# Low-part transposes and row scatters of a chunk, put off by one to three steps, in a scan with a mixture of experts

## The chip, the cores and the metric

One core of one Trainium2 chip. The metric is the device time of one execution in microseconds; the time of a kernel is the median of its runs.

## The reference

`x` and `f_logit` are 4 x 5056 x 256. A gated scan runs along each sequence, and its output goes token by token (20,224 of them) through one of eight experts, the one with the largest gate logit:

```python
f = lower_bound + (1 - lower_bound) * sigmoid(f_logit)
h = f[:, t] * h + (1 - f[:, t]) * x[:, t]          # for each t: y[:, t] = h
logits = y @ w_gate                                # 20224 x 8
e = argmax(logits)
gate_w = softmax(logits)[e];  eom = sigmoid(y @ w_output_gate)[e]
out = gate_w * eom * (relu(y @ w1[e]) @ w2[e])     # w1[e]: 256 x 1024, w2[e]: 1024 x 256
```

## The kernel before

**Chunks.** The tokens are taken in 40 chunks of 512 (`chunk`, L259; the last has 256). `load_chunk` (L246) puts f and x, channels on partitions, into two tiles `ft` and `xt`, of which there are two each in turn (`XB`). A chunk computes tanh on ScalarE (L270), the scan on VectorE (L285), a scale, then splits the scanned rows into a high (L315) and a low (L319) fp16 part, both written over `ft`. `turn(i, k)` (L310) issues a DMA transpose on SP's queue that puts 128 channels of one part into `rows`, tokens on partitions: two for the high part (L323), two for the low part (L343). Small matmuls (L334) give the gate logits; VectorE finds each token's expert and its place in that expert's list (L350 to L421) and the factor (L435). Then four indirect DMAs on POOL's queue (L438), one per 128 tokens, scatter the rows to `scr` in device memory, sorted by expert.

**Tiles.** `plan` (L481) turns the counts of tokens already sent into tiles of 256 rows of one expert, whose place and expert are known only at run time. `gather` (L631) fetches one such tile by a DMA transpose on SP into `xq` (L638) and its places and factors into `mt` (L641). `gemm1` (L681) multiplies with w1 in three fp16 products (L690 to L692), `low` (L698) makes the low part of the hidden values on VectorE, `gemm2` (L708) multiplies with w2 (L730 to L732), `evacuate` (L767) scales on ScalarE (L776) and `put` (L778) scatters the result to `out` on POOL (L780). Before these run-time tiles, while the weights are still being prepared, there are sixteen early tiles of known expert.

**The order of the work.** It is written out by hand. `chunk` is a generator; a bare `yield` ends its work for one step, a yield of `SMALL` or `BIG` only lets other work of the same step in between (`together`, L158). `pump` (L841) runs one step: it begins a new chunk every eight steps (`PERIOD`), moves every live chunk one step on, the oldest first, together with the work of the tile, and at most one plan. `experts` (L975) has four quarters to a tile of 256 rows, and each makes one step. `ahead` (L871), called at a tile's first quarter, sees that the next tile is planned and gathered; if no rows are known it plans at once. A chunk counts as sent when its last scatter is issued (`state["sent"]`, L443). `loading` (L799) issues the loads of the next chunk after a chunk's fifth bare yield. `aside` and `beside` (L232, L237) put the chunk's small matmuls between the tile's.

`between["on"]` is set (L1020) when the run-time tiles begin. From there on `ordered` (L965) keeps every engine's instructions in the order in which they are written. SP's queue is in that order throughout. A DMA waits only for what its data need, so before the change a transpose goes when its part is written, and the scatters one after another when the places are known.

Of the kernel before, what the change touches and what calls it, by code (L numbers as in the profile page):

```python
# [12 lines left out]
I16 = mybir.dt.int16  # L13
# [7 lines left out]
DATA = mybir.DependencyInfo(mybir.DependencyClass.Sync, mybir.DependencyReason.DATA)  # L21
# [17 lines left out]
PUMPS0 = 3.0  # L39
TURN = 3  # L40
XB = 2
DRAIN = 1.25
REST = 6

# [6 lines left out]
def raw(ins):  # L51
    return getattr(ins, "ins", ins)
# [3 lines left out]
def tile_scan_moe(  # L56
# [10 lines left out]
    nc = tc.nc  # L67
    P = 128
    D, N = xT.shape
    KD = D // P  # L70
# [18 lines left out]
    def sure(tokens):  # L89
# [19 lines left out]
        out=tri, in_=ones, compare_op=ALU.is_gt, fill=0.0, base=0, pattern=[[1, P]], channel_multiplier=-1  # L109
# [63 lines left out]
    def alone(g):  # L173
# [12 lines left out]
        out=gsq, in0=wgf, scalar=1.0, in1=wgf, op0=ALU.mult, op1=ALU.mult, accum_out=gss  # L186
# [9 lines left out]
        out=wgs[:, :, 1, :], in0=wgc, scalar=gsc, in1=wgs[:, :, 0, :], op0=ALU.mult, op1=ALU.subtract  # L196
# [5 lines left out]
    def apart(ins, group, keep=()):  # L202
        tc.declare_no_dep(raw(ins), group=group, keep=[raw(k) for k in keep], reason="rows apart")
        tc.add_to_no_dep_group(group, raw(ins))
# [25 lines left out]
    between = {"on": False}  # L230

    def aside(f, *a):  # L232
        queue.append((f, a))
        if not between["on"]:
            beside()
# [10 lines left out]
    def load_chunk(c):  # L246
# [5 lines left out]
        else:  # L252
            ft = p1.tile([P, KD, CH], F32, tag="ft", name="ft", bufs=XB)
            xt = p1.tile([P, KD, CH], F32, tag="xt", name="xt", bufs=XB)
        nc.sync.dma_start(out=ft[:, :, 0:n], in_=fv_in[:, :, t0 : t0 + n])
        nc.sync.dma_start(out=xt[:, :, 0:n], in_=xv_in[:, :, t0 : t0 + n])
        loaded[c] = (xt, ft)

    def chunk(c):  # L259

        t0 = c * CH
        n = min(CH, N - t0)
        nb = n // P
# [8 lines left out]
        for k in range(KD):  # L272
            yield BIG
            nc.vector.scalar_tensor_tensor(
                out=h[k], in0=f[k], scalar=1.0, in1=h[k], op0=ALU.subtract, op1=ALU.mult
# [5 lines left out]
        for k in range(KD):  # L281
            for a, z in zip(cuts[:-1], cuts[1:]):
# [3 lines left out]
                    out=xt[:, k, a:z], data0=ft[:, k, a:z], data1=xt[:, k, a:z], initial=init, op0=ALU.mult, op1=ALU.add  # L286
# [19 lines left out]
        hl = ft.rearrange("p k n -> p (k n)").bitcast(F16).rearrange("p (i k n) -> p i k n", i=2, k=KD)  # L306
        rows = row2[c % 2] if c else row0
        assert c < 3 or c - 2 in state

        def turn(i, k):  # L310
            q = i * KD + k
            nc.sync.dma_start_transpose(out=rows[:, 0:nb, q * P : (q + 1) * P], in_=hl[:, i, k, 0:n].bitcast(I16))

        for k in range(KD):
            nc.scalar.activation(hl[:, 0, k, 0:n], xt[:, k, 0:n], AF.Copy, scale=sa[:, k : k + 1])  # L315
# [1 line left out]
        for k in range(KD):  # L317
            yield BIG
            nc.vector.scalar_tensor_tensor(  # L319
                out=hl[:, 1, k, 0:n], in0=xt[:, k, 0:n], scalar=sa[:, k : k + 1], in1=hl[:, 0, k, 0:n],  # L320
                op0=ALU.mult, op1=ALU.subtract,
            )
            turn(0, k)  # L323
# [15 lines left out]
        for b in range(nb):  # L339
            for i in range(2):  # L340
                aside(gates, i, b)
        for k in range(KD):
            turn(1, k)  # L343
        yield
        lgp = sp.tile([P, NB, 2 * G], F32, tag="lgp", name="lgp")
        nc.scalar.activation(lgp[:, 0:nb], pr[:, 0:nb], AF.Copy, scale=li)
        yield
        lgo = sp.tile([P, NB, G], F32, tag="lgo", name="lgo")
        yield SMALL
        nc.vector.tensor_tensor(out=lgo[:, 0:nb], in0=lgp[:, 0:nb, 0:G], in1=lgp[:, 0:nb, G : 2 * G], op=ALU.add)  # L350
# [6 lines left out]
        def small(nm, w=None, dt=F32):  # L357
# [11 lines left out]
            out=key[:, 0:nb], in0=dl[:, 0:nb], scalar=0.0, in1=rev.unsqueeze(1).to_broadcast([P, nb, E]),  # L369
# [26 lines left out]
        for s in range(nb + 1):  # L396
# [12 lines left out]
            out=pos[:, 0:nb], in0=pk[:, 0:w].rearrange("p (b e) -> p b e", e=E),  # L409
# [10 lines left out]
        with nc.allow_low_precision("whole numbers"):  # L420
# [9 lines left out]
            out=fc[:, 0:nb], in0=es[:, 0:nb], scalar=1e-9, in1=eg[:, 0:nb], op0=ALU.add, op1=ALU.mult  # L430
# [4 lines left out]
        nc.vector.tensor_scalar(meta[:, :, 0:2].bitcast(F32), fc[:, 0:nb].unsqueeze(2), ix, None, ALU.mult)  # L435
        yield
        for b in range(nb):
            ins = nc.gpsimd.indirect_dma_start(  # L438
                out=scr[:, :], out_offset=IOA(ap=dst[:, b : b + 1], axis=0), in_=rows[:, b, :], in_offset=None
            )  # L440
            apart(ins, "scr")
            fresh.append(ins)
        state["sent"] = cn  # L443
# [355 lines left out]
    def loading(c):  # L799

        at = 0
        for kind in chunk(c):
            if not kind:
                at += 1
                if at == LOADAT and EARLY[0] <= c + 1 < NCH:
                    load_chunk(c + 1)
            yield kind

    def plans(need):
# [12 lines left out]
        if c == NCH:  # L822
            prog["final"] = True
            planning.append(plan(WHOLE, P, P // 2 - 1, "whole"))
            for nm, of in (("hh", "ft"), ("hl", "xt")):
                z = p1.tile([P, KD, CH], F32, tag=of, name=of, bufs=XB).rearrange("p k n -> p (k n)").bitcast(F16)
                z = z.rearrange("p (j i n) -> p j i n", i=2, n=P)
# [32 lines left out]
    def step(k, tasks, need=PLAN):  # L860
        prog["left"] += k
        if prog["left"] < 1.0:
            together(tasks)
        while prog["left"] >= 1.0:
            prog["left"] -= 1.0
            pump(tasks, need)
            tasks = []
# [15 lines left out]
    turns = [0] * len(EARLY)  # L883

    def early(j):

        if not line or line[0]["half"] == 1 and len(line) == 1:
            for r in range(len(firsts)):
                e = turns[r]
                if e < min(E, (j + 1) // 2) and (r == 0 or e < turns[r - 1]):  # L890
                    T = gather(f"f{r * E + e}", firsts[r][e], e)
                    T["half"] = 0
                    line.append(T)
                    turns[r] += 1
                    break
        tasks, wait, ready, late = [], list(pend), list(over), list(mid)
        pend.clear()
        over.clear()
        mid.clear()
        for T, h in wait:  # L900
            tasks.append(first_low(T, h))
            if h == 0:
                tasks.append(factors(T))
        go = line and line[0]["ev"] < j // 2

        def rest():
            for T in ready:
                evacuate(T)
                put(T)
            if go:  # L910
                T, h = line[0], line[0]["half"]
                T["half"] += 1
                if h == 1:
                    line.pop(0)
                first1(T, h)
                pend.append((T, h))
            for T, h in late:
                first2(T, h)
                if h == 1:
                    over.append(T)  # L920
            mid.extend(wait)

        return tasks, rest
# [31 lines left out]
    while turns[-1] < E or line or pend or mid or over:  # L955
        mine, rest = early(nh)
        step(DRAIN, mine, LEAD)
        rest()
# [16 lines left out]
    def experts(t0, t1, more, late=0, rest=None):  # L975
# [3 lines left out]
        for t in range(t0, t1 + 2):  # L979
# [4 lines left out]
            for q in range(4):  # L984
# [12 lines left out]
                if T and t == end - 1 and q % 2:  # L997
                    if q == 1:
                        T["w2"] = [
                            p1.tile([P, KD, CH], F32, tag=of, name=of, bufs=XB).rearrange("p k n -> p (k n)").bitcast(F16)  # L1000
                            for of in ("ft", "xt")
# [74 lines left out]
```

## Time and profile before

| | us |
|---|---|
| median of 3 runs | 999.99 |
| lowest, highest | 997.69, 1004.57 |
| the profiled execution | 999.55 |
| its span, from the first to the last instruction | 997.8 |
| TensorE, VectorE, ScalarE, GpSimd (POOL) busy in it | 913.4, 799.1, 510.8, 361.1 |

Times in the rows are counted from the span's start. A matmul's end is modelled, and matmuls overlap: in a dense row of them one of 256 columns starts every 0.11 us and is shown as 0.27 us long. An idle time in brackets counts from the end of the row before.

### The profile page before, as it was taken

Reading aid. Unit: us, or ns where it says so; the run is one execution under the profiler, and the core shown is the slowest. Engines: PE = TensorE matmul, PEld = TensorE weight load, DVE = VectorE, ACT = ScalarE, POOL = GpSimd, SP = SyncE. Lnnn points to the kernel's source line nnn. Section 1 sums busy time; section 2 is a strip of 40 time slices with the busy share of each in tenths; the row PEclk is TensorE's granted clock in tenths of the full one; section 3 lists DMA queues with packets and bytes.
Section 4 is the critical chain, followed back from the end, with each engine's and each line's share of the span. In section 5 each row is a group of like instructions: output and inputs, shape, how many; then the busy total and the mean of one; then the engine's idle time right before and its main releaser. Section 6 shows DMA issues by size and latency. Waiting matters only on the chain.

```text
span 997.8 us, 30899 instructions
## 1 busy us (share of the span) xinstructions
PE 913.4 (92%) x9775; PEld 817.2 (82%) x9775; DVE 799.1 (80%) x2683; ACT 510.8 (51%) x1075; POOL 361.1 (36%) x380
## 2 busy tenths in 40 slices
PE   2257888999999999999999999999999999999997
PEld 2247868788888888888888888888888888899996
DVE  7978867697888888888888888888888886836653
ACT  6666656454655554555555555545555453333332
POOL 1432324243433434443334444333434343321112
PEclk9669989999999999999999999999999999999999
DMA  8899973886666557567656666656566653232211
GB/s 306 205 272 268 256 199 110 156 174 146 139 152 160 135 151 138 154 146 149 161 132 149 146 155 149 154 144 138 134 152 143 153 126 82 72 88 46 52 34 34
DMA packets 236526, 146.15 MB, mean 146 GB/s; under 512 B 200507, under 2 KB 202172, under 8 KB 236368
## 3 DMA queue, kind: packets, MB, share of 16 engines
q1 hardware_dynamic: 220784, 101.34, 45.9%
q0 software_dynamic: 15296, 42.73, 14.5%
q8 instruction: 93, 1.52, 0.6%
q14 instruction: 65, 0.53, 0.2%
q10 hardware_dynamic: 288, 0.02, 0.0%
HBM read 58.38 MB, written 44.23 MB: 103 GB/s over the span
## 4 chain that ended last, share of the span: by engine, by line
PE 74%; issue 10%; DMA 8%; DVE 4%; POOL 2%; SPq 1%; ACT 0%; another core or an unknown queue 0%; POOLq 0%; DVEq 0%; ACTq 0%
PE ph L690 11%; PE py L730 11%; PE ph L691 11%; PE ph L692 11%; PE py L732 11%; PE py L731 11%; DMA out_dram<-yo,mt 3%; DMA xq<-scr 3%; POOL out_dram L780 2%; PE ph L743 1%; PE ph L744 1%; PE ph L745 1%; PE pr L334 1%; DMA w<-in_wT_dram 1%; PE py L764 1%
## 5 line engine op out<-in xcount | busy, mean ns | idle before, releaser
L695 ACT ACTIVATE hh<-ph 128x512 f16<-128x512 f32 (+1 forms) x312 | 173.3, 556 | 309.9 <-PE ph L692 246.3
L690 PE MATMUL ph<-xq,w 128*128 128x256 f16 (+2 forms) x1312 | 326.1, 259 | 3.2 <-DVE fac L657 2.2
L691 PE MATMUL ph<-xq,w 128*128 128x256 f16 (+2 forms) x1312 | 326.3, 259 | 1.5 <-issue 1.3
L692 PE MATMUL ph<-xq,w 128*128 128x256 f16 (+2 forms) x1312 | 326.6, 259 | 0.7 <-issue 0.4
L730 PE MATMUL py<-w2s,hh 128*128 x1136 | 309.0, 272 | 2.5 <-issue 2.0
L731 PE MATMUL py<-w2s,hh 128*128 x1136 | 309.2, 272 | 0.5 <-issue 0.5
L732 PE MATMUL py<-w2s,hl 128*128 x1136 | 309.3, 272 | 0.0
L780 POOL DMA_INDIRECT out_dram<-yo,mt x146 | 150.3, 1029 | 384.5 <-ACT yo L776 340.0
L703 DVE SCALAR_TENSOR_TENSOR hl<-ph,hh 128x512 f16<-128x512 f32 (+1 forms) x312 | 198.6, 636 | 46.6 <-ACT hh L695 35.9
L438 POOL DMA_INDIRECT scr<-rows,dst x154 | 177.6, 1154 | 142.4 <-issue 128.5
L665 DVE COPY w<-w1s 128x2048 f16 x164 | 114.2, 697 | 51.8 <-PE ph L692 37.5
L690 PEld LDWEIGHTS <-w 128*128 128x128 f16 x1312 | 127.6, 97 | 15.8 <-DVE fac L657 2.5
L692 PEld LDWEIGHTS <-w 128*128 128x128 f16 x1312 | 127.3, 97 | 13.9 <-issue 2.2
L691 PEld LDWEIGHTS <-w 128*128 128x128 f16 x1312 | 127.3, 97 | 11.7 <-issue 2.1
L732 PEld LDWEIGHTS <-hl 128*128 128x128 f16 x1136 | 110.7, 97 | 14.7 <-issue 0.6
L730 PEld LDWEIGHTS <-hh 128*128 128x128 f16 x1136 | 110.8, 98 | 13.7 <-issue 1.7
L731 PEld LDWEIGHTS <-hh 128*128 128x128 f16 x1136 | 110.7, 97 | 11.4 <-issue 0.5
L285 DVE TENSOR_TENSOR_SCAN xt<-ft,xt 128x512 f32<-128x512 f32 (+4 forms) x78 | 92.5, 1195 | 0.3
L776 ACT ACTIVATE yo<-py,fac 128x256 f32<-128x256 f32 (+1 forms) x146 | 62.0, 469 | 30.3 <-PE py L732 25.3
L315 ACT ACTIVATE ft<-xt,sa 128x512 f16<-128x512 f32 (+1 forms) x76 | 50.2, 708 | 43.2 <-DVE pos L408 23.1
L319 DVE SCALAR_TENSOR_TENSOR ft<-xt,sa,ft 128x512 f16<-128x512 f32 (+1 forms) x76 | 56.1, 742 | 20.0 <-ACT ft L270 18.1
L334 PEld LDWEIGHTS <-ft 128*128 128x128 f16 x600 | 51.2, 98 | 17.9 <-ACT ft L315 5.0
(189 smaller groups left out, 1364.6 us busy)
## 6 DMA issues: line engine op xcount, KB each, us to landing
ft<-in_fT_dram SPq DMA_DIRECT2D x37, 512.0 KB
xt<-in_xT_dram SPq DMA_DIRECT2D x37, 512.0 KB
w<-in_wT_dram SPq DMA_DIRECT2D x32, 512.0 KB
scr<-rows,dst POOLq DMA_INDIRECT x154
rows<-ft SPq DMA_TRANSPOSE x152
out_dram<-yo,mt POOLq DMA_INDIRECT x146
xq<-scr SPq DMA_TRANSPOSE x98
scr<-padt SPq DMA_DIRECT2D x9, 136.0 KB
```

Source lines behind the costliest of these rows:

```text
L285: nc.vector.tensor_tensor_scan(out=xt[:, k, a:z], data0=ft[:, k, a:z], data1=xt[:, k, a:z], initial=init, op0=ALU.mult, op1=ALU.add)
L438: ins = nc.gpsimd.indirect_dma_start(out=scr[:, :], out_offset=IOA(ap=dst[:, b : b + 1], axis=0), in_=rows[:, b, :], in_offset=None)
L665: nc.vector.tensor_copy(out=w, in_=w1f[:, ds(T["ev"] * (2 * WH) + h * 2 * QH, 2 * QH)])
L690: nc.tensor.matmul(out=o, lhsT=w[:, f, k, 0, :], rhs=T["xh"][:, k, 0:n], start=first, stop=False)
L691: nc.tensor.matmul(out=o, lhsT=w[:, f, k, 0, :], rhs=T["xl"][:, k, 0:n], start=False, stop=False)
L692: nc.tensor.matmul(out=o, lhsT=w[:, f, k, 1, :], rhs=T["xh"][:, k, 0:n], start=False, stop=last)
L695: nc.scalar.activation(hh[:, :, 0:n], ph[:, :, 0:n], AF.Relu)
L703: nc.vector.scalar_tensor_tensor(out=hl[:, :, 0:n], in0=ph[:, :, 0:n], scalar=0.0, in1=hh[:, :, 0:n], op0=ALU.max, op1=ALU.subtract)
L730: nc.tensor.matmul(out=o, lhsT=hh[:, i, c], rhs=wh, start=first, stop=False, skip_group_check=True)
L731: nc.tensor.matmul(out=o, lhsT=hh[:, i, c], rhs=wl, start=False, stop=False, skip_group_check=True)
L732: nc.tensor.matmul(out=o, lhsT=hl[:, i, c], rhs=wh, start=False, stop=last, skip_group_check=True)
L780: ins = nc.gpsimd.indirect_dma_start(out=out[:, :], out_offset=IOA(ap=T["mt"][0 : T["p"], b, 2:4].bitcast(I32), axis=0), in_=T["yo"][0 : T ...
```

## The change

From the run-time tiles on, the two transposes of the low part are issued two steps later (step 12 of the chunk instead of 10, where steps are counted by bare yields from 0), and the second, third and fourth scatter one, two and three steps later. Each of these five DMAs is given a dependency (`pace`) on the VectorE instruction written last before it, so that it can't go earlier than that step. Chunks whose steps lie before `between["on"]` are as they were.

```diff
+SPLIT = (1, 2, 3)
+LATER = (12, 12)
...
+    def pace(ins):
+
+        if between["on"]:
+            last = next(i for i in reversed(nc.cur_bb.bb.instructions) if i.engine == nc.vector.engine)
+            tc.add_manual_dep(raw(ins), last.name, DATA, reason="pace")
...
         for b in range(nb):
             for i in range(2):
                 aside(gates, i, b)
-        for k in range(KD):
-            turn(1, k)
-        yield
+        when = LATER if between["on"] else (10, 10)
+
+        def turns(stage):
+            for k in range(KD):
+                if when[k] == stage:
+                    pace(turn(1, k))
+
+        turns(10)
+        yield
+        turns(11)
         lgp = sp.tile([P, NB, 2 * G], F32, tag="lgp", name="lgp")
         nc.scalar.activation(lgp[:, 0:nb], pr[:, 0:nb], AF.Copy, scale=li)
         yield
+        turns(12)
         lgo = sp.tile([P, NB, G], F32, tag="lgo", name="lgo")
...
         for b in range(nb):
+            if between["on"] and b in SPLIT:
+                yield
             ins = nc.gpsimd.indirect_dma_start(
                 out=scr[:, :], out_offset=IOA(ap=dst[:, b : b + 1], axis=0), in_=rows[:, b, :], in_offset=None
             )
+            if b in SPLIT:
+                pace(ins)
             apart(ins, "scr")
             fresh.append(ins)
```

`turn` returns the DMA that it issues, for `pace`.

## Rows read from the trace of the kernel before

**Rows 1.** The page's busy us, share of the span and count, whole span.

```profile
PE 913.4 (92%) x9775; PEld 817.2 (82%) x9775; DVE 799.1 (80%) x2683; ACT 510.8 (51%) x1075; POOL 361.1 (36%) x380
```

**Rows 2.** Windows of two tiles: length, busy us (count), clock, DMA share, GB/s.

```profile
224.35:247.43 23.08, 22.14 (x218) 19.54 (x216) 18.90 (x63) 11.71 (x25) 8.24 (x9) 1.00 0.66 141
...
489.18:511.48 22.30, 21.81 (x217) 19.34 (x215) 19.37 (x65) 11.69 (x26) 9.20 (x10) 1.00 0.60 154
511.48:533.02 21.54, 21.54 (x217) 19.32 (x215) 19.00 (x64) 12.10 (x27) 8.75 (x10) 1.00 0.67 145
...
685.19:708.78 23.59, 22.46 (x218) 19.18 (x216) 19.64 (x65) 11.26 (x24) 10.26 (x10) 1.00 0.60 144
...
839.98:862.30 22.32, 21.79 (x206) 19.14 (x203) 14.78 (x59) 7.24 (x16) 8.40 (x10) 1.00 0.33 87
sum 637.95, PE 630.69 PEld 560.61 DVE 542.53 ACT 330.83 POOL 259.69; mean PE 21.75 PEld 19.33 DVE 18.71 ACT 11.41 POOL 8.95
```

**Rows 3.** The same view, one window cut at its second tile.

```profile
489.18:500.87 11.69, 11.20 (x116) 9.84 (x114) 9.99 (x30) 6.74 (x16) 3.36 (x4) 1.00 0.67 178
500.87:511.48 10.61, 10.61 (x103) 9.50 (x101) 9.38 (x36) 4.95 (x10) 5.84 (x6) 1.00 0.53 128
```

**Rows 4.** Time line of TensorE: start, us, engine, line, operation, [idle before, releaser].

```profile
490.69 0.27 PE L730 MATMUL py<-w2s,hh 128*128 x1
491.45 0.27 PE L731 MATMUL py<-w2s,hh 128*128 x1 [0.49 <-issue]
```

**Rows 5.** Time line of SP's queue, one chunk.

```profile
487.43 0.95 SPq L638 DMA_TRANSPOSE xq<-scr  x1
...
489.15 2.56 SPq L312 DMA_TRANSPOSE rows<-ft  x2
493.35 0.38 SPq L255 DMA_DIRECT2D ft<-in_fT_dram  x1
495.00 0.38 SPq L256 DMA_DIRECT2D xt<-in_xT_dram  x1
502.40 1.12 SPq L638 DMA_TRANSPOSE xq<-scr  x1
...
505.04 2.53 SPq L312 DMA_TRANSPOSE rows<-ft  x2
```

**Rows 6.** Time line of POOL, the same chunk.

```profile
485.05 1.45 POOL L438 DMA_INDIRECT scr<-rows,dst  x1 [3.15 <-issue]
...
489.39 1.20 POOL L438 DMA_INDIRECT scr<-rows,dst  x1 [0.30 <-issue]
492.41 1.00 POOL L780 DMA_INDIRECT out_dram<-yo,mt  x1 [1.83 <-ACT yo L776]
```

**Rows 7.** Windows of two us over the same chunk.

```profile
485.18:487.18 2.00, 2.00 (x21) 1.80 (x19) 2.00 (x4) 0.63 (x2) 1.70 (x2) 1.00 0.64 150
...
489.18:491.18 2.00, 1.78 (x23) 1.51 (x21) 1.67 (x4) 1.40 (x3) 1.20 (x1) 1.00 1.07 231
...
495.18:497.18 2.00, 2.00 (x21) 1.79 (x19) 1.77 (x6) 1.84 (x6) 0.00 (x0) 1.00 0.92 299
...
499.18:501.18 2.00, 2.00 (x21) 1.79 (x19) 1.71 (x11) 0.91 (x4) 0.00 (x0) 1.00 0.05 16
```

**Rows 8.** Time line of VectorE, the same chunk.

```profile
488.78 0.68 DVE L274 SCALAR_TENSOR_TENSOR xt<-ft,xt 128x512 f32<-128x512 f32 x1
...
490.41 0.69 DVE L703 SCALAR_TENSOR_TENSOR hl<-ph,hh 128x512 f16<-128x512 f32 x1
...
493.63 1.34 DVE L285 TENSOR_TENSOR_SCAN xt<-ft,xt 128x512 f32<-128x512 f32 x1
...
498.63 0.16 DVE L490 TENSOR_TENSOR pl_n<-cnt,boff 128x8 f32<-128x8 f32 x1
```

**Rows 9.** Time line of ScalarE, the tanh.

```profile
506.00 1.14 ACT L270 ACTIVATE ft<-ft 128x512 f32<-128x512 f32 x2
```

More of the change, by code (lines that the diff above doesn't have):

```diff
@@ L311, in turn @@
             q = i * KD + k
-            nc.sync.dma_start_transpose(out=rows[:, 0:nb, q * P : (q + 1) * P], in_=hl[:, i, k, 0:n].bitcast(I16))
+            return nc.sync.dma_start_transpose(
+                out=rows[:, 0:nb, q * P : (q + 1) * P], in_=hl[:, i, k, 0:n].bitcast(I16)
+            )
         for k in range(KD):
```

## The prediction

> **What bounds the kernel now.** I read the shares of busy time first, then cut the stretch with run-time tiles into windows, then read four queues over one chunk.
>
> TensorE is busy 913.4 of the 997.8 us and VectorE 799.1 [rows 1]. Such a mean mixes a start that waits for data with a long stretch that doesn't, so I cut from the first matmul (L690) of every second tile to that of the second next: one window holds two tiles of 256 rows, and one chunk is handed through in it. From 224.35 to 862.30 us there are 29 windows, 637.95 us together [rows 2]. With nearly the same number of matmuls (217 or 218; 206 in the last) their lengths differ: the shortest is 21.54 us and stands in ten of them, and in it TensorE is busy for the whole 21.54. The longest is 23.59. If all 29 took 21.54, the sum would be 29 x 21.54 = 624.7 us. So this stretch holds 637.95 - 624.7 = 13.3 us that isn't matmul work, and nothing that leaves the matmuls alone can win more in it than that. VectorE has some 19 us of work in a window, 2.5 less than the floor, so it doesn't set the floor.
>
> Where do the 13.3 us lie? One of the long windows, cut at its second tile: the first ("even") tile takes 11.69 us with TensorE idle for 0.49 of them, the second ("odd") 10.61 with none [rows 3]. Odd tiles take 10.61 throughout; quiet even ones take 10.93, since they carry the chunk's gate matmuls. All the loss is in even tiles. On the engine's own time line it is this: an L730 matmul starts at 490.69 and the L731 behind it at 491.45 instead of 0.11 later. The idle time is put down to "issue", to no engine and no transfer [rows 4]. Most such gaps start within 3 us of the start of an even tile. What is under way then? On SP, tile rows are gathered at 487.43 and the two low-part transposes issued at 489.15 [rows 5]; on POOL the four row scatters run from 485.05 to 490.6 [rows 6]; the DMA engines are full, 1.07 in the two us from 489.18, against 0.64 four us earlier, where the high-part transposes were on their way [rows 7]. From 499.18 they stand almost idle, 0.05.
>
> **The change part by part.** No arithmetic is added or removed. What moves is counted in steps, a quarter tile, some 2.7 us each (10.61 / 4). Counting the bare yields of a chunk, its transposes of the low part stand in step 10 and move to 12, and its scatters stand in step 16, of which three move to 17, 18 and 19. A new chunk begins every 8 steps, so step 12 of one is step 4 of the next.
>
> *The two transposes.* They now wait for the last VectorE instruction written before step 12. That stands right behind the second scan of the next chunk, which ends at 493.63 + 1.34 = 494.97 [rows 8]. So they go from 489.15 to about 495.0: 5.8 us later, into a stretch without scatters. They last 2.5 us in the queue as before.
>
> *What is queued behind them on SP.* Nothing is overtaken: the next entries are the loads of f and x two chunks ahead, at 493.35 and 495.00 [rows 5]. The f load writes the tile that the transposes read, so it waits for their landing. Before, the transposes' issue ended at 489.15 + 2.56 = 491.71 and the load went 1.64 later. After: 495.0 + 2.56 + 1.64 = 499.2 for f and, half a us on, 499.7 for x. The old loads were over by 499.18, when the rate falls to 16 GB/s [rows 7]: at most 4.2 us after x was issued. So the new ones are in at about 504. They are read by the tanh of that chunk at 506.00 on ScalarE [rows 9]: 2 us to spare. The next gather stands behind the loads and goes at 502.40 anyway [rows 5], for a plan whose VectorE work starts at 498.63 [rows 8]; it may be slowed by the tail of the loads, by at most the 1.6 us from 502.4 to 504. Its tile starts at 511.48 [rows 2], so this is hidden. Cost: nothing, covered by 2 us for the load and the 9.1 from issue to use for the gather; if the first cover goes, see the second rival.
>
> *The three scatters.* The first stays at 485.05. The others wait for the last VectorE instruction of one step each: the second for the residual that follows the gather's copies, near 487.5; the third for the end of L274, 488.78 + 0.68 = 489.5; the fourth for L703, 490.41 + 0.69 = 491.1 [rows 8]. The fourth was at 489.39, so the last one is 1.7 us later, and with its 1.20 us it ends at 492.3. Behind it on POOL stands the output scatter L780, which starts at 492.41 after waiting for ScalarE [rows 6]. Cost: 0 to 0.1 us for POOL, and nothing on the path.
>
> *The plan.* A chunk is counted as sent only when its last scatter is issued, now step 19 instead of 16. The plan that uses it stands ahead of step 22, with its first instruction at 498.63, 7.5 us behind the new last scatter [rows 8]. So no extra step is forced anywhere, and the last chunk only shortens its lead. Cost: nothing.
>
> *What is won.* The burst loses two of its transposes and is thinner in the scatters. The trace doesn't show a window with this order, so I bound it by windows that exist. Best: every window like the one of 511.48, -13.3 us. No gain: 0. Worst: the burst only moves and each window becomes like that of 489.18, 22.30, or 29 x 0.76 = 22.0 us over the floor, which is +8.7 against now. I take two thirds of the best, -8.9 us: the transposes are what lies across the gaps and they leave; but one gather and the scatters stay, and some gaps start later in the tile. The value lies nearer to the quiet rows because those are ten of 29 with the burst in place, so little has to be taken off for the rest to be quiet too.
>
> The Trainium skill has a rule that speaks against this: by "SBUF — State Buffer", section "SBUF: two separate sides", the engines and the DMA engines reach that memory by separate sides and don't contend. By it no transfer could hold a matmul, the gaps would have another cause and the sum would be 0. The trace gives idle time beside full DMA engines but names no releaser, so it doesn't decide; the same full share at the loads, 0.92 from 495.18 [rows 7], goes with no gap, which is for the rule.
>
> **Sum.** The profiled execution took 999.55 us, with a span of 997.8. 999.55 - 8.9 = 990.7; the median of the three runs is 0.4 above it, so 991.
>
> **Rivals.**
>
> 1. *The gaps stay.* They come from the gate matmuls or from TensorE's own supply of instructions, and the transposes were beside them by chance. For it: "issue" as the named cause, ten quiet windows with the same burst, loads without gaps. Against it: odd tiles never have them. The time is then that of before, 999 to 1001.
>
> 2. *The load comes too late, and the kernel is slower.* The place is ScalarE's tanh at 506.00, price as follows. The new waits close a ring: scan, transposes, load, tanh, scan of the next chunk. Now the scan ends at 494.97 and the tanh is 11.0 us behind, of which the new chain takes 9.0 by the sum above (4.2 + 4.8). From 2 us more than that on, every further us stretches the window. If the two landings are 3 us slower in all, each window gains 1 us: 29 us, 1029. VectorE's 2.5 us of spare time could soften it, since VectorE is itself in the ring; I don't count on that. For it: the load now runs beside a gather and output scatters. Against it: the DMA engines are idle there (0.05).
> The Trainium skill's page "DMA: Bandwidth & Descriptors", section "Queues, rings and completion order", has each DMA engine take a queue's descriptors in ring order; by it the gather would stand behind the whole load, which is the 1.6 us above, and no run here shows it apart.
>
> 3. *The burst moves into odd tiles.* Load tail, gather, high-part transposes at 505.04 and the first scatter come closer together. Then the gaps come there: the bound above, +8.7, so 1008.
>
> 4. *All of it goes:* 999.99 - 13.3 = 986.7.
>
> **How the numbers follow.** The forecast, most gaps gone, has 0.50 and its own range is 987 to 996. The first rival has 0.30, the second 0.05, the third 0.08, the fourth 0.07. The range of 985 to 1005 takes in the forecast, the fourth and the first rival and leaves out the second, most of the third and some width at both ends. One per cent, about what a measurement tells from no change, is 10 us. Faster by more: of the forecast the part below 990, two fifths, 0.20, and the fourth, together 0.27. Slower by more: the second, and of the third the half above 1010, 0.09. Within: 0.64.
>
> **What would show it.** Right: windows of two tiles near 21.6 to 21.8 on average instead of 22.0; SP's low-part transposes right behind the second scan; the f load some 6 us later relative to its tile; even tiles near 10.93. Wrong: the transposes moved and even tiles as long as before (first rival); ScalarE waiting for the f load ahead of L270 (second); odd tiles above 10.61 (third). A time above 1005 would say that I mis-sized the 2 us of cover.

## The result and the profile after

The kernel after takes 988.12 us (median of four runs, 985.57 to 991.65), the kernel before beside it 1000.29 (997.69 to 1004.57): a ratio of 0.9896, with an interval of 0.9863 to 0.9929. The profiled execution took 989.18 us, with a span of 987.5. One thing has to be known for all that follows: the kernel before itself took 1000.3, 994.1 and 993.2 us in three measurements and 976.4 and 975.9 in two others, so ratios are compared within a measurement. The ratios and intervals are those that each measurement gave; they differ by up to 0.3% from the quotients of the medians (here 0.988). Two slow runs, one of 1201.65 us of the kernel with the transposes alone and one of 1001.77 us of the kernel before in its repeat, are left out.

The page's busy line of the kernel after, against [rows 1]. TensorE's count is the same, its busy time 5.6 us less; POOL's busy time has risen by 21.4 us with the same count.

```profile
PE 907.8 (92%) x9775; PEld 815.4 (83%) x9775; DVE 796.7 (81%) x2683; ACT 513.0 (52%) x1075; POOL 382.5 (39%) x380
```

Windows of two tiles of the kernel after (columns as in [rows 2]):

```profile
219.98:241.52 21.54, 21.54 (x218) 19.30 (x216) 19.59 (x66) 12.11 (x26) 10.73 (x10) 1.00 0.66 157
...
414.61:436.90 22.29, 21.86 (x217) 19.24 (x215) 18.11 (x63) 11.63 (x26) 9.32 (x9) 1.00 0.64 154
...
479.98:501.52 21.54, 21.54 (x217) 19.32 (x215) 19.60 (x66) 12.08 (x26) 10.70 (x10) 1.00 0.60 156
...
803.80:826.98 23.18, 22.24 (x218) 19.31 (x216) 16.37 (x62) 8.88 (x22) 8.77 (x10) 1.00 0.40 88
826.98:849.68 22.70, 21.86 (x205) 18.85 (x203) 13.69 (x51) 6.74 (x15) 9.71 (x11) 1.00 0.35 91
sum 629.70, PE 626.64 PEld 559.63 DVE 540.26 ACT 332.21 POOL 282.83; mean PE 21.61 PEld 19.30 DVE 18.63 ACT 11.46 POOL 9.75
```

Of the 29 windows 24 now stand at 21.54; five are longer, at 22.26 to 23.18. The sum is 629.70 against 637.95, and 629.70 - 624.66 = 5.0 us are left over the floor where there were 13.3. The same view, the window of 479.98 cut at its second tile, against [rows 3]:

```profile
479.98:490.91 10.93, 10.93 (x116) 9.82 (x114) 10.04 (x30) 6.09 (x15) 5.75 (x6) 1.00 0.52 145
490.91:501.52 10.61, 10.61 (x103) 9.50 (x101) 9.56 (x37) 6.00 (x11) 4.95 (x4) 1.00 0.69 168
```

The even tile has lost the 0.76 us that it had over 10.93; the odd one is as before. The gaps that remain are of the same kind as [rows 4], but lie later, 3 to 5.8 us into an even tile. Time line of TensorE, kernel after; the tile began at 414.61, and the first line is its last gate matmul, 2.4 us ahead of the gap:

```profile
417.58 0.20 PE L344 MATMUL pr<-wgs,ft 128*128 128x16 f16 x2
...
420.35 0.27 PE L752 MATMUL py<-w2s,hh 128*128 x1 [0.36 <-issue]
```

Where did the span's 10.3 us go? Cut at the first run-time tile (194.90 before, 191.27 after), at the first window (224.35 and 219.98) and at the last window's end (862.30 and 849.68): -3.6 us before any run-time tile, -0.7 in the first three tiles, -8.25 in the 29 windows, and +2.3 behind them (135.5 before, 137.8 after; 1.8 of it is one wait of the first gemm1 product for a gather). The first of these cannot be the change's, since that part of the kernel is the same. The last did not come again: a repeat of the kernel after (below) had 135.6 there.

Now the queues. SP's time line in the kernel after, against [rows 5]; L320 is `turn`, L257 and L258 the loads, L660 and L663 the gather; the even tile begins at 479.98:

```profile
477.86 1.29 SPq L660 DMA_TRANSPOSE xq<-scr  x1
...
483.67 2.56 SPq L320 DMA_TRANSPOSE rows<-ft  x2
488.01 0.38 SPq L257 DMA_DIRECT2D ft<-in_fT_dram  x1
488.49 0.42 SPq L258 DMA_DIRECT2D xt<-in_xT_dram  x1
493.13 1.65 SPq L660 DMA_TRANSPOSE xq<-scr  x1
...
495.56 2.53 SPq L320 DMA_TRANSPOSE rows<-ft  x2
```

Relative to the tile, the low-part transposes go at +3.7 us (before: 0.0), the f load at +8.0 (before: +4.2); the medians over the 29 even tiles are +3.6 (before: -0.7) and +8.2 (+4.2). What they wait for stands in SP's waits from 250 to 480 us (engine, line, releaser: us in total, times, longest):

```profile
SPq L320 <- DVEq L672: 41.9, 11, 4.7
...
SPq L257 <- DMA rows<-ft: 19.2, 10, 3.3
```

L672 is the load of a register with the tile's expert, issued from VectorE's queue: that was the VectorE instruction written last, not the scan. The second scan of the next chunk, whose end I had taken for it, is written a step ahead of the register load and yet only starts as the transposes go. VectorE's and ScalarE's time lines, that scan and the tanh behind the load:

```profile
483.70 1.27 DVE L293 TENSOR_TENSOR_SCAN xt<-ft,xt 128x512 f32<-128x512 f32 x1
```
```profile
496.19 1.14 ACT L278 ACTIVATE ft<-ft 128x512 f32<-128x512 f32 x2
```

The tanh follows 8.2 us behind the f load's issue, and ScalarE doesn't wait for it. POOL's time line, against [rows 6]; L458 are the scatters of rows, L802 that of the output:

```profile
476.42 1.43 POOL L458 DMA_INDIRECT scr<-rows,dst  x1 [3.80 <-issue]
479.15 1.29 POOL L458 DMA_INDIRECT scr<-rows,dst  x1 [1.30 <-DVE fac L679]
481.08 1.16 POOL L458 DMA_INDIRECT scr<-rows,dst  x1 [0.64 <-DVE xt L282]
482.55 1.42 POOL L458 DMA_INDIRECT scr<-rows,dst  x1 [0.30 <-issue]
484.27 1.54 POOL L802 DMA_INDIRECT out_dram<-yo,mt  x1 [0.31 <-issue]
```

The second and the third scatter now stand apart from the one ahead; the fourth goes 0.30 us behind the third, as soon as POOL is free, at +2.6 (before: +0.2). The output's scatter now waits for POOL and goes at +4.3 instead of +3.2.

### The profile page after: what moved, and what is told of

Same layout as the page of the kernel before. It is cut to its first block, busy times and chain, and to the rows that moved or that the text cites. A ratio compares the mean times of both kernels' runs of the same rounds, so it can differ in the third digit from the quotient of the medians.

```text
span 987.5 us, 30990 instructions
## 1 busy us (share of the span) xinstructions
PE 907.8 (92%) x9775; PEld 815.4 (83%) x9775; DVE 796.7 (81%) x2683; ACT 513.0 (52%) x1075; POOL 382.5 (39%) x380
## 4 chain that ended last, share of the span: by engine, by line
PE 71%; issue 10%; DMA 9%; DVE 5%; POOL 2%; SPq 2%; ACT 1%; POOLq 0%; another core or an unknown queue 0%; DVEq 0%; ACTq 0%
PE ph L712 11%; PE py L752 11%; PE ph L714 11%; PE py L754 11%; PE ph L713 11%; PE py L753 11%; DMA xq<-scr 3%; DMA out_dram<-yo,mt 3%; POOL out_dram L802 2%; DVE xt L293 1%; DMA w<-in_wT_dram 1%; PE ph L765 1%; PE pr L344 1%; PE ph L766 1%; PE ph L767 1%
## 5 line engine op out<-in xcount | busy, mean ns | idle before, releaser
L802 POOL DMA_INDIRECT out_dram<-yo,mt x146 | 155.5, 1065 | 309.2 <-ACT yo L798 256.1
L458 POOL DMA_INDIRECT scr<-rows,dst x154 | 193.2, 1254 | 186.8 <-issue 116.1
```

Of the source, the lines that this page charges most:

```text
L458: ins = nc.gpsimd.indirect_dma_start(out=scr[:, :], out_offset=IOA(ap=dst[:, b : b + 1], axis=0), in_=rows[:, b, :], in_offset=None)
L802: ins = nc.gpsimd.indirect_dma_start(out=out[:, :], out_offset=IOA(ap=T["mt"][0 : T["p"], b, 2:4].bitcast(I32), axis=0), in_=T["yo"][0 : T ...
```

## The experiments

The theories, by the letters of the expectations. A: it is the transposes that lie across the matmuls together with the scatters, and moving them is what wins. B: it is the four scatters one behind the other. C: the transposes hurt because they read the tile that the gate matmuls read. E: transfers run slower on some chips, and only there are gaps and a gain. F: the difference between measurements is one of speed alone, and the change is worth nothing. In all figures below "over the floor" is the length of the same 29 windows less 29 x 21.54 = 624.66 us. A sum may fall 0.3 below that: the last window has 205 or 206 matmuls instead of 217, and without a gap it takes 21.24, as in the kernel after in its second profile (further down), so that the least sum is 28 x 21.54 + 21.24 = 624.36.

```profile
822.51:843.75 21.24, 21.24 (x206) 19.03 (x203) 13.42 (x53) 6.96 (x15) 8.88 (x10) 1.00 0.32 84
```

### Each half alone, no waits, and a pair put back: no gaps to be seen

Transposes alone moved, then scatters alone:

```diff
-SPLIT = (1, 2, 3)
+SPLIT = ()
```

> The changed kernel, with the four row scatters again in one step and without waits: only the two low-part transposes are put off. Theory A (the low-part transposes, issued among the scatters, go with the gaps in the matmuls): nearly the whole gain stays, 987 to 992 us, and the windows of two tiles sum to some 630 us. Theory B (four scatters back to back do it): the gain is lost, 996 to 1001. Theory C (it is the transposes, but because they read the tile whose columns the gate matmuls load at the same time): as A.

```diff
-LATER = (12, 12)
+LATER = (10, 10)
```

> The changed kernel, with the two low-part transposes in step 10 as before: only three scatters are put off. Theory A: most of the gain is lost, 995 to 1001 us. Theory B: the gain stays, 986 to 991. Theory C: as A.

The code in its new places, but without the dependencies:

```diff
-        if between["on"]:
+        if between["on"] and WAITS:
```

> The changed kernel, with the five DMAs written in the later steps but without the added waits on VectorE. All theories: nothing stands between the old and the new place on SP's queue or POOL's, so both run as early as before, and the time is that of before, 996 to 1002 us. If it is below 992, the place in the written order counts and not the wait.

The kernel after with two transposes put back into step 10 that have nothing to do with the chunk; they read weights in `w2s` and write a tile that nobody reads:

```diff
         turns(10)
+        if between["on"]:
+            plain = w2f[:, 0 : KD * CH].bitcast(I16).rearrange("p (k n) -> p k n", k=KD)
+            spare = mpool["m"].tile([P, NB, KD * P], I16, tag="spare", name="spare", bufs=1)
+            for k in range(KD):
+                nc.sync.dma_start_transpose(out=spare[:, 0:nb, k * P : (k + 1) * P], in_=plain[:, k, 0:n])
```

> The changed kernel, with two more transposes in step 10, where the low-part ones stood before. They read a piece of the finished w2 weights and write to a tile that nobody reads, so the output is as before. Theory A: transposes among the scatters bring the gaps back, 994 to 1002 us, the gaps in the first 3 us of even tiles. Theory B: 986 to 991, as the scatters stay spread. Theory C: 986 to 991, since the tile that the gate matmuls read isn't touched.

| | us | before, beside it | ratio, interval |
|---|---|---|---|
| transposes alone | 975.58 | 976.36 | 0.9993, 0.9968 to 1.0017 |
| scatters alone | 976.68 | 976.36 | 1.0013, 0.9993 to 1.0033 |
| no dependencies | 976.62 | 976.36 | 1.0003, 0.9982 to 1.0025 |
| after, and an extra pair | 976.42 | 976.36 | 1.0007, 0.9985 to 1.0030 |

None differs from the kernel before, and the times expected above are all missed: here there is nothing to win. All 29 windows as one, of the kernel with the transposes alone:

```profile
214.71:839.07 624.36, 624.36 (x6226) 560.02 (x6224) 548.53 (x1827) 334.94 (x713) 296.77 (x262) 1.00 0.59 145
```

TensorE is busy for the whole 624.36 us. The other kernels of this measurement had 624.4 to 624.5 too, also the one without dependencies, whose burst is in its old place. (The kernel before wasn't profiled here; that it has no gaps either is taken from that kernel and from its time.) One thing these runs do show: where the DMAs go without the dependencies. SP's and POOL's time lines of that kernel; the even tile begins at 491.58:

```profile
488.22 1.25 SPq L661 DMA_TRANSPOSE xq<-scr  x1
...
490.24 2.53 SPq L321 DMA_TRANSPOSE rows<-ft  x2
```
```profile
486.67 1.45 POOL L459 DMA_INDIRECT scr<-rows,dst  x1 [2.45 <-issue]
488.42 0.96 POOL L459 DMA_INDIRECT scr<-rows,dst  x1 [0.30 <-issue]
489.68 1.02 POOL L459 DMA_INDIRECT scr<-rows,dst  x1 [0.30 <-issue]
491.01 1.49 POOL L459 DMA_INDIRECT scr<-rows,dst  x1 [0.30 <-issue]
```

They go at -1.3 and at -4.9 to -0.6, at least as early as before the change. So writing the DMAs later doesn't put them later; the five dependencies do it.

### Both kernels again

> The changed kernel as it is, once more, beside the kernel before on one chip. Theory A (the moved transposes free the matmuls from gaps of some 10 us): about 10 us faster than before, wherever it runs, ratio 0.987 to 0.993. Theory E (the gaps come only where a chip's transfers run slower, and the change is worth something there alone): where the kernel before takes some 976 us, as on the chip of the first four experiments, no difference, ratio 0.998 to 1.003; where it takes some 1000, about 0.99. Theory F (the two kernels were measured on chips of different speed and the change is worth nothing): ratio 0.998 to 1.003 on any chip.

> The kernel before as it is, for its profile on the chip of this comparison. Theory A: windows of two tiles that sum to some 638 us, as in the first profile, with the gaps in even tiles. Theory E: gaps only if its time is near 1000 us; if it is near 976, every window takes 21.54 us. Theory F: the same as E here; the two differ by the changed kernel beside it.

No edits. The kernel after: 985.81 against 994.05, ratio 0.9943 (0.9917 to 0.9969). The kernel before against itself: 992.64, ratio 0.9982 (0.9955 to 1.0009). The 29 windows as one, after and then before:

```profile
217.03:843.75 626.72, 625.38 (x6226) 559.69 (x6223) 540.01 (x1822) 333.36 (x713) 280.56 (x264) 1.00 0.59 145
```
```profile
220.02:852.48 632.46, 628.41 (x6226) 561.03 (x6223) 543.39 (x1828) 330.61 (x714) 260.24 (x263) 1.00 0.62 144
```

Over the floor stand 2.1 us after and 7.8 before. Where the gaps exist the change takes most of them, and the 5.7 us between the two stretches are most of the 6.8 between the two medians. F falls, and so does A's "wherever it runs". Of E the observation holds, a gain only where there are gaps, but not the reason given: this measurement and the first four experiments both name chip 2, and transfers weren't slower where there are gaps. The kernel with the transposes alone has a DMA share of 0.59 without gaps (above) and 0.58 with them (below).

### The parts again, where there are gaps

The edits are those above; the last is the kernel after once more, as the measure for the others.

> Only the two transposes put off, again, since the first four experiments ran where the kernel before had no gaps. If it takes some 990 us or more this time: theory A, the whole gain of the changed kernel beside it (ratio 0.990 to 0.996); theory B, none (0.998 to 1.002). If the kernel before takes some 976 again: no difference, and nothing told apart.

> Only the three scatters put off, again. Where the kernel before takes some 990 us or more: theory A, ratio 0.998 to 1.002; theory B, the whole gain, 0.990 to 0.996; both halves of the change needed: 0.998 to 1.002 here and in the kernel with the transposes alone.

> The changed kernel with two unrelated transposes back in step 10, again. Where the kernel before takes some 990 us or more: theory A, the gain is gone, ratio 0.997 to 1.003, gaps again in the first 3 us of even tiles; theories B and C, the gain stays, 0.990 to 0.996.

> The changed kernel on the same chip, as the measure for the other three. Where the kernel before takes some 990 us or more: ratio 0.990 to 0.996. Where it takes some 976: 0.998 to 1.002, which would be theory E; under theory A it would be 0.99 there too.

| | us | before, beside it | ratio, interval | over the floor, us |
|---|---|---|---|---|
| transposes alone | 988.91 | 993.19 | 0.9967, 0.9942 to 0.9991 | 5.1 |
| scatters alone | 989.10 | 993.19 | 0.9968, 0.9946 to 0.9990 | 4.1 |
| after, and an extra pair | 991.75 | 993.19 | 0.9989, 0.9964 to 1.0015 | 9.4 |
| after | 984.73 | 993.19 | 0.9924, 0.9888 to 0.9960 | 1.6 |

The last column is from one profiled execution each, and such figures scatter: the kernel before had 13.3 and 7.8 in its two. The 29 windows as one, in the order of the table:

```profile
218.22:847.95 629.73, 627.63 (x6226) 560.40 (x6224) 544.04 (x1826) 331.40 (x714) 261.44 (x262) 1.00 0.58 144
```
```profile
219.96:848.69 628.73, 626.11 (x6225) 559.95 (x6223) 540.34 (x1822) 332.98 (x713) 280.74 (x264) 1.00 0.58 145
```
```profile
220.39:854.49 634.10, 628.89 (x6226) 559.37 (x6224) 540.82 (x1820) 332.51 (x713) 285.23 (x264) 1.00 0.66 155
```
```profile
219.16:845.40 626.24, 625.21 (x6225) 559.97 (x6223) 538.39 (x1821) 333.87 (x713) 280.83 (x263) 1.00 0.59 145
```

Each half alone wins a third of a per cent, both together 0.76: about the sum, though the intervals of one half and of both overlap. So neither A nor B alone is right; each half thins the burst, and each counts. (With the scatters alone the transposes keep their dependency, in step 10, and go at +0.3 us in the median against -0.7 before; so that half isn't quite pure.) The extra pair, which leaves the dependencies and all the chunk's own DMAs as in the kernel after, takes the gain back: 7.0 us between the medians, 9.4 us over the floor, and no measurable difference from before. The tile of the gate matmuls isn't read by that pair, so C falls as the reason for the loss. (The pair reads `w2s`, which the gemm2 products read too; whether a pair that reads a tile that no matmul reads does the same was not tried.)

The gaps of the kernel with the extra pair didn't lie in the first 3 us of even tiles but mostly 4 to 6 us into them. SP's time line and TensorE's gaps there; L364 is the extra pair:

```profile
481.99 2.53 SPq L364 DMA_TRANSPOSE spare<-w2s  x2
486.88 2.51 SPq L320 DMA_TRANSPOSE rows<-ft  x2
```
```profile
487.76 0.27 PE L757 MATMUL py<-w2s,hh 128*128 x1 [0.34 <-issue]
488.54 0.27 PE L758 MATMUL py<-w2s,hh 128*128 x1 [0.17 <-issue]
489.24 0.27 PE L757 MATMUL py<-w2s,hh 128*128 x1 [0.33 <-issue]
```

They fall beside the chunk's own low-part transposes, behind the extra pair and the scatters, not beside the extra pair itself. In the kernel with the transposes alone the gaps lie the other way round, 0.9 to 3.8 us into even tiles, beside scatters and with no low-part transpose under way. One of them, in the tile that begins at 455.92, TensorE's and POOL's time lines; the low-part transposes go at 461.29:

```profile
457.26 0.28 PE L714 MATMUL ph<-xq,w 128*128 128x256 f16 x1 [0.21 <-issue]
```
```profile
454.06 0.96 POOL L458 DMA_INDIRECT scr<-rows,dst  x1 [0.30 <-issue]
455.33 0.96 POOL L458 DMA_INDIRECT scr<-rows,dst  x1 [0.31 <-issue]
```

So the gaps aren't tied to one kind of transfer. That they follow the amount that is crowded together fits all these runs but isn't shown by itself, and why they come this late in the crowd is open.

### The gate matmuls moved, and the dependencies again

For the first rival of the prediction, the gate matmuls were moved out of the burst instead: the kernel before, with the low-part transposes left where they were and the gate matmuls and all that follows two steps later.

```diff
+        for k in range(KD):
+            turn(1, k)
+        if between["on"]:
+            yield
+            yield
         for b in range(nb):
             for i in range(2):
                 aside(gates, i, b)
-        for k in range(KD):
-            turn(1, k)
         yield
```

> The kernel before, with the chunk's small gate matmuls, and all of the chunk that follows them, two steps later; the low-part transposes stay in step 10, and the scatters come at the start of even tiles. So the transfers are as dense there as before, but no gate matmuls lie among the large ones. Where the kernel before takes some 990 us or more: if dense transfers alone make the gaps, they stay in the first 3 us of even tiles, ratio 0.998 to 1.004; if the gate matmuls are needed as well, the gaps vanish or move to some 5 us into the tile, where the gates are now, and the ratio is 0.990 to 0.997. Where it takes some 976: 0.998 to 1.003, and nothing told apart.

> The changed kernel without the five waits, again. In the first of these runs its transposes and scatters went as early as in the kernel before. Where that takes some 990 us or more, the time should be that of before, ratio 0.998 to 1.002, under every theory in which the place of the transfers counts; if it is 0.990 to 0.996, the later place in the written order counts by itself.

This measurement was again one without gaps (before: 975.86). The gates kernel took 982.83, ratio 1.0066 (1.0039 to 1.0092), above the 0.998 to 1.003 expected, and the one without dependencies 975.14, ratio 0.9996 (0.9978 to 1.0014). The kernel without dependencies was never measured where there are gaps, so that the dependencies bring the gain is shown by where the DMAs go and not by a time. Its 29 windows as one:

```profile
211.56:836.06 624.50, 624.50 (x6226) 560.03 (x6223) 545.79 (x1820) 335.60 (x713) 293.80 (x262) 1.00 0.60 145
```

The gates kernel had 624.36 there, so it says nothing of the gaps. It shows something else: a chunk that is two steps longer throughout costs at its end. Behind the last window it took 139.5 us where the kernel without dependencies takes 135.5, and most of that is one wait of TensorE for the gather of a late tile (waits of TensorE from 830 to 970 us). Another 2.4 us lie ahead of the windows, which begin at 213.9 against 211.6; these are not explained.

```profile
PE ph L693 <- DMA xq<-scr: 3.4, 1, 3.4
```

In the kernel after only the DMAs are later, not the computation of places, and that cost doesn't come regularly: 1.8 us in the first profile, none in the two repeats, and about as much again with the scatters alone and with the extra pair (137.6 and 137.4 us behind the last window).

## Why the prediction was right, and where it was off

**The bound.** It held but for 0.3 us. The floor of 21.54 us for two tiles stands in all kernels, no window of 217 or 218 matmuls went below it, and the gain came out of the time over it, in even tiles. The last window, with 206, I had counted like the others; it can take 21.24, so 13.6 us stood to be won and not 13.3.

**The two transposes.** Expected 5.8 us later, measured 3.7. The step that failed is "That stands right behind the second scan of the next chunk": what counts is the register load written last, and it was done before that scan, written ahead of it, had begun (the transposes go at 483.67, the scan at 483.70). The size of the move was off, its direction not.

**What is queued behind them.** Nothing was overtaken, and the f load waited for the landing of the transposes, as said. It went 3.9 us later relative to its tile instead of 5.8 (4.17 to 8.03), and 8.2 us lay between its issue and the tanh instead of the 6.8 of my sum, so the cover was larger than the 2 us I gave it. The second rival's ring never closed.

**The three scatters.** The fourth was expected 1.7 us later; in the chunk shown it is 2.4 later and in the median of the 29 tiles 1.9. It went when POOL was done with the third, not when its own dependency was met. "Cost 0 to 0.1 us for POOL" was too small: the output scatter starts 1.1 us later relative to its tile. That nothing on the path sees it was right.

**The plan.** No wait of TensorE stood out in the run-time stretch but one of 1.1 us for a gather, ahead of the windows; "cost: nothing" was right for the windows. The end of the kernel I hadn't looked at, and there a lead that is shorter can show.

**What is won.** -8.9 us was predicted for the 29 windows, -8.25 measured: 62% of the loss where I took two thirds. In the repeat it was 5.7 of 7.8, or 73%. That is the right term with about the right size, for a reason that the runs bear out: a crowd put back takes the gain away. But two thirds was a guess, and how close -8.25 comes to it is partly luck, since the loss itself was 13.3 us in one profile of the kernel before and 7.8 in the other. And the prediction gave the gain to the transposes, as "what lies across the gaps"; the scatters are worth as much (0.9968 against 0.9967). The total fits less well than it seems. Of the 12.2 us between the medians the windows explain 8.25; 3.6 us of the profiled difference were won ahead of the change, by which the two executions simply differ. What the change is worth is told better by all three ratios, 0.9896, 0.9943 and 0.9924, together with "nothing" where the kernel before has no gaps.

**The rule against it.** By the Trainium skill, "SBUF — State Buffer", section "SBUF: two separate sides", the engines and the DMA engines don't contend, and the sum would have been 0. The measurements without gaps agree: there the same crowd costs nothing. Those with gaps don't: an unrelated pair of transposes brings back 7.8 us (9.4 - 1.6) of time over the floor, and 7.0 between the medians. No run tells by which way, so the rule isn't refuted as to the memory itself; it can't be used, though, to put the cost of DMAs beside matmuls at zero.

**The rivals.** The first, that the gaps stay, fell in this measurement; its thought that the cause is TensorE's own supply of instructions isn't excluded. That instructions are loaded too late is unlikely, though: of the 86 gaps named "issue" from 215 us on in the eight profiles that have gaps, 9 overlap a packet of the page's larger instruction queue (q8), which has one in flight 11% of the time, so no more than chance gives, and none overlaps a packet of the smaller (q14). The second showed no trace: no wait of ScalarE ahead of L278 from 200 us on. The third neither: the odd tile shown takes 10.61, and the long windows lose in their even tiles. The fourth asked for too much; 1.6 to 5.0 us stay.

**What stays open.** What makes the matmuls wait in some measurements and not in others, with the same code and the clock granted in full (1.00, that is the 2.4 GHz level, in every window of either kind): the trace names no releaser. Whether the gate matmuls are needed for it: in the kernel after most gaps lie 1.9 us and more behind the last of them, so they need not stand beside the gap; but every gap lies in a tile that carries them, behind the first. And why, where there are gaps, the last window but one stays 1.4 to 2.3 us over the floor in the kernels whose scatters are spread (1.64 in the window of 803.80).

## What to carry to other kernels

Where TensorE sets the pace, compare windows of equal work with the shortest of them: the sum over that floor bounds what moving transfers can win, before anything is built. To spread DMAs out it isn't enough to write them later; each needs a dependency, and one should look in the trace at which instruction that lands on. And measure and profile the kernel before several times: the gaps that this change removes were there in three measurements and absent in two.

## What was not expected of the hardware

The same code ran in 976 us in some measurements and in 993 to 1000 in others. The difference lies not only in the gaps (next to none in the kernels profiled there, against 7.8 and 13.3 us in the windows of the kernel before) but also ahead of the run-time tiles: the 29 windows begin at 211.6 to 214.7 us in the kernels shown from the former and at 217.0 to 224.4 in those from the latter. The granted clock doesn't explain it: it is 1.00 in every window of either kind, and over whole runs 0.965 to 0.995 with gaps and 0.97 to 0.998 without. And gaps that carry the name "issue" answered to DMA traffic: with two transposes more per chunk (0.66 against 0.59 of the DMA engines' time) they grew from 1.6 to 9.4 us over the floor.
